# Gated mix of local attention and a squared-ReLU MLP: later row tiles of the first tokens loaded through ScalarE's queue, products over two token tiles in turn, no products on zeros

## The chip, the core and the metric

The kernel runs on one core of one Trainium2 chip. The metric is device time in microseconds: the median of several runs. One further execution is taken with the hardware profiler; its rows are what the text reads. PE is TensorE's matmul row, PEld its weight loads, DVE VectorE, ACT ScalarE, POOL GpSimd, SP SyncE.

## What is computed

For 2048 tokens of width 448 (float32) the reference mixes two branches with a gate per token:

```python
g = sigmoid((x * gate_w).sum(-1))
q, k, v = split(x @ wqkv)            # 16 heads of 28
a = softmax(q . k[pos - 2*j], j = 0..7) weighted v, @ wo     # window 8, dilation 2
b = relu(x @ w1 + b1)**2 @ w2 + b2   # 1792 hidden
out = g * a + (1 - g) * b
```

## The kernel before

Products are to be more exact than one pass of TensorE's fast float32 form (fp32r) gives. So every operand is split into a high part, rounded to fp32r, and a low part, the rest: `split_full` (L114) has ScalarE write the high part (L115) and VectorE subtract it for the low part (L116). A product of two operands is then three matmuls: high x high, high x low, low x high.

The 448 rows of the contraction are three row tiles of 128 (k = 0, 1, 2) and a last one of 64 that is held twice, in partitions 0 to 63 and 64 to 127. Tokens come transposed, in four chunks of 512 (`CH`), each of four token tiles of 128 (i = 0 to 3). The order on every engine is written out by hand; a planner's clock (`advance`, `at`, `when`) hands out splits, loads, stores and attention pieces as the products go on. A part of the work on one engine stands in a queue and waits in order.

The stretch that matters here is the start, up to the first 16 us:

- L103 clears one element (`none`), L618 a tile of zeros, and L620 runs 13 products (`WARM`) on these zeros.
- L625 to L632 issue the loads of the first chunk and its query weights, all on SP's queue. For each k: the weights' row tile (`wqraw0`, L627; 128 x 450, 450 because two columns of the gate stand beside the 448), then the tokens' row tile (`xraw0`, L632; 128 x 512, for k = 0 in two halves of 256 columns). For the last row tile the weights come in two parts (L630). Then come the weights of keys and values (L637, L640) and the second chunk (L554).
- L642 to L652 split what lands. For k = 0, 1, 2 ScalarE rounds the weights (L643, `wqh`), VectorE rounds the tokens (L645) and makes the weights' low part (L646, `wql`) and the tokens' low part (L647). For k = 0 the second half of the tokens is rounded by ScalarE (L649), with its low part on VectorE (L650). The last row tile goes through `split_full` (L115, L116).
- `qkv_first` (L246) then has the first query products. For each k and each token tile i it issues the three matmuls of that tile (L253): high x wqh, high x wql, low x wqh, all into the accumulator of tile i. Behind the twelve products of k it issues `FILL[k]` = 2, 1, 0 products on the zeros (L256). Everything later runs as pairs of 64 rows side by side (L184, `side_by_side`), first with the last row tile, for queries and keys.

The DMAs of the program take their completion semaphores in turn out of eight. So a ninth and a tenth load wait, before they are issued, for an earlier load with the same semaphore to land.

`none` (L102) is also the source of small ScalarE copies that let the next accumulation pass between the two halves of the rows (`turn`, L192).

Of the kernel before, what the change touches and what calls it, by code (L numbers as in the profile page):

```python
# [9 lines left out]
AF = mybir.ActivationFunctionType  # L10
# [4 lines left out]
P = 128  # L15
# [7 lines left out]
CH = 512  # L23
NQ = D + 2
# [23 lines left out]
DEFER = 2  # L48
ORDER = (3, 0, 1, 2)
WARM = 13  # L50
FILL = (2, 1, 0)
PP_BUFS = 4
ST_BUFS = 3
BT_BUFS = 8
# [3 lines left out]
def gated_mix_kernel(ctx: ExitStack, tc: tile.TileContext, xT, wqkv, w1, w2, wo, b1, b2, out):  # L58
    nc = tc.nc

    def f32(ap):
        return ap.bitcast(F32)
# [37 lines left out]
    biasp = ctx.enter_context(tc.tile_pool(name="biasp", bufs=1))  # L100
    b1z = biasp.tile([P, 16], F32, name="b1z")
    b1t, none = b1z[:, :NF], b1z[0:1, 15:16]  # L102
    nc.vector.memset(none, 0.0)  # L103

    ctx.enter_context(tc.manual_schedule())
    nc.gpsimd.memset(mask, 0.0)
# [24 lines left out]
    def x_tiles(c, pool):  # L131
        return X([pool.tile([P, 2, CH], F32R, tag=f"x{j}", name=f"x{c}_{j}") for j in range(4)])
# [9 lines left out]
    def ps(tag, name):  # L142
        return psum.tile([P, 512], F32, tag=tag, name=name, bufs=4)
# [20 lines left out]
    def block(b):  # L164

        o = (0, NP, NP + D)[b]
        return slice(o, o + ncols(b))
# [45 lines left out]
    def full(x, acc, tl, b, ks=range(3)):  # L213
        sl, n = slice(tl * P, tl * P + P), block(b)
        r = []
        for k in ks:
            r += [(acc, x.h[k][:, sl], wqh[:, k, n]), (acc, x.h[k][:, sl], wql[:, k, n]),
                  (acc, x.l[k][:, sl], wqh[:, k, n])]
        return r

    def last(x, acc, tl, b):

        sl = slice(tl * P, tl * P + P)
        n = block(1) if b == 2 else slice(0, ncols(b))
        h, l = w7h[:, n], w7l[:, n]
        return [(acc, x.x7[:, sl], h), (acc, x.x7[:, sl], l), (acc, x.x8[:, sl], h)]

    def accs(c, b, tls, tags):
        return [Acc(t, f"qkv{c}_{tl}_{b}", ncols(b)) for t, tl in zip(tags, tls)]

    def run(c, todo, steps):


        a = 0
        for e, done, *turns in steps:
            side_by_side(todo[0][a:e], todo[1][a:e])
            while a < e:
                advance(min(12, e - a) * MM448)
                a = min(a + 12, e)
            for t in turns:  # L240
                t() if callable(t) else turn(*t)
            for b, tl, acc in done:
                assert acc.todo == 0
                qkv_evacuate(acc.pt, c, tl, b)

    def qkv_first(x):  # L246

        four = range(4)
        q = accs(0, 0, four, "bbbb")
        for k in range(3):  # L250
            for i in four:
                for j, (acc, a, w) in enumerate(full(x, q[i], i, 0, (k,))):
                    nc.tensor.matmul(acc.pt[:, :NQ], a, w, start=k == j == 0, stop=False)  # L253
            advance(12 * MM448)
            for _ in range(FILL[k]):
                nc.tensor.matmul(warm[:, :2 * P], zero[:, :P], zero, start=True, stop=True)  # L256
        for acc in q:
            acc.todo = 3
        k = accs(0, 1, four, "mmmm")
        t = [sum((last(x, a[i], i, b) for i in four), []) for b, a in ((0, q), (1, k))]  # L260
        f = [full(x, k[i], i, 1) for i in four]
        run(0, [t[0] + f[0] + f[1] + f[2] + f[3], t[1] + f[2] + f[3] + f[0] + f[1]],
            [(3, [(0, 0, q[0])], (k[0], k[0])),
             (12, [(0, i, q[i]) for i in (1, 2, 3)], (k[1], k[1])),
             (24, [], (k[0], k[2])), (33, [], (k[1], k[3])),
             (39, [(1, 0, k[0]), (1, 2, k[2])]), (48, [(1, 1, k[1]), (1, 3, k[3])])])
        v = accs(0, 2, four, "bbbb")
        f, l = [full(x, v[i], i, 2) for i in four], [last(x, v[i], i, 2) for i in four]
        run(0, [f[0] + l[0] + f[2] + l[2] + f[1] + f[3], f[1] + l[1] + f[3] + l[3] + f[0] + f[2]],
            [(15, [], (v[0], v[1])), (24, [], (v[2], v[3])),  # L270
             (33, [(2, 0, v[0]), (2, 1, v[1])]), (42, [(2, 2, v[2]), (2, 3, v[3])])])
# [195 lines left out]
    def advance(dt):  # L467
        clock["pe"] += dt
        while due := [x for x in later if x[0] <= clock["pe"]]:
            item = min(due, key=lambda x: x[0])  # L470
            later.remove(item)
            item[1]()
        if not clock["on"]:
            clock["att"] = clock["pe"]
            return
        while clock["att"] < clock["pe"]:
            try:
                r = next(att)
            except StopIteration:
                clock["on"] = False  # L480
                return
            if r is None:
                clock["att"] = clock["pe"]
                return
            clock["att"] += r


    def raw_tile(name):
        return rawp.tile([P, 4, 512], F32, tag="raw", name=name)
# [126 lines left out]
    warm = ps("m", "warm")  # L616
    zero = prodp.tile([P, 2 * P], F32R, tag="pp", name="zero", bufs=PP_BUFS)
    nc.vector.memset(f32(zero), 0.0)  # L618
    for _ in range(WARM):
        nc.tensor.matmul(warm[:, :2 * P], zero[:, :P], zero, start=True, stop=True)  # L620

# [2 lines left out]
    rx = raw_tile("xraw0")  # L624
    for k in range(4):  # L625
        if k < 3:
            nc.sync.dma_start(raws[0][:, k, :NQ], wqkv[0, :, k])  # L627
        else:
            for b, rows in ((0, slice(0, 64)), (1, slice(64, P))):
                nc.sync.dma_start(raws[0][rows, k, :NQ], wqkv[b, rows, k])  # L630
        for cols in ((slice(0, 256), slice(256, CH)) if k == 0 else (slice(0, CH),)):
            nc.sync.dma_start(rx[:, k, cols], xT[0, :, k, cols])  # L632

    for b, tag in ((1, "k"), (2, "v")):
        raw = attp.tile([P, 3, D], F32, tag=tag, name=f"wqraw{b}")
# [5 lines left out]
    x = x_tiles(0, xap)  # L641
# [77 lines left out]
    for c in range(4):  # L719
        x = xs[c]  # L720
        if c == 0:
            qkv_first(x)
        else:
            qkv_two(x, c, 0, copies=c == 3)
            qkv_two(x, c, 2, (mlp_one, mlp_two) if c == 3 else (), c == 3)
        if c == 1:
            st_["spilled"] = 0
            clock["on"] = True
            clock["att"] = clock["pe"] - 1.0
            advance(0.0)  # L730
        if c == 3:
            st_["spilled"] = 1
# [266 lines left out]
    for g in range(2, 2 * NF):  # L999
        i, f = g // (NF // 2), g % (NF // 2) * 2  # L1000
# [4 lines left out]
        if not f:  # L1005
            x, slots = X([nxt[j][0] for j in range(4)]), [nxt[j][1] for j in range(4)]
# [111 lines left out]
```

## Time and profile before

| | us |
|---|---|
| median of 3 runs | 418.29 (418.14 to 418.49) |
| the profiled execution | 418.03 |
| its span, first to last instruction | 416.1 |
| PE busy | 409.4 |
| DVE, ACT, POOL busy | 256.0, 207.8, 268.7 |
| first product of real data starts (L253) | 4.74 |
| first product of L184 starts | 13.57 |

Times in the views are counted from the span's start. A matmul's busy time overlaps with the next one's, so the distance from start to start tells the pace, not the mean duration. A row of the timeline has the start, the duration, engine, line, operation, out<-in, shape and count; in brackets how long the engine was idle before it and what ended the wait. A row of the view of windows has the busy time of PE, PEld, DVE, ACT and POOL in the stretch, then the granted clock of TensorE, the mean busy share of the core's 16 DMA engines, and GB/s.

### The profile page before, as it was taken

What the parts mean: (1) busy time and instruction counts of PE and PEld (TensorE: products, weight loads), DVE (VectorE), ACT (ScalarE), POOL (GpSimd) and SP (SyncE); (2) the same over time, 40 slices, a digit from 0 to 9 for tenths busy, and PEclk for the clock granted to TensorE, in tenths of its full rate; (3) what the DMA queues carried; (4) which work ended last, traced back from release to release, by engine and by line L of the source; (5) the groups of instructions that cost most, each with busy time, mean ns of one, the idle gap of its engine ahead of it and who ended that gap; (6) DMA issues with size and microseconds to landing.
All of it is one profiled execution on the core that took longest, in us unless ns stands there. A gap on an engine that the chain in (4) does not pass through costs nothing.

```text
span 416.1 us, 9332 instructions
## 1 busy us (share of the span) xinstructions
PE 409.4 (98%) x3844; PEld 377.4 (91%) x3844; DVE 256.0 (62%) x403; ACT 207.8 (50%) x471; POOL 268.7 (65%) x167
## 2 busy tenths in 40 slices
PE   8999999999999999999999999999999999999995
PEld 7999999999999999888888888989898888888994
DVE  4520522276676767777656797879586677882343
ACT  3641655288766565444565535444653253346630
POOL 0000000874988999999989898999899986940000
PEclk9999999999999999999999999999999999999999
DMA  7999799979164307554112659765146512178204
GB/s 227 359 339 317 225 365 284 366 248 329 48 204 177 127 2 256 207 183 150 30 56 100 223 162 260 195 145 149 33 154 199 213 46 84 51 184 129 83 2 177
DMA packets 65323, 73.76 MB, mean 177 GB/s; under 512 B 32320, under 2 KB 58368, under 8 KB 64896
## 3 DMA queue, kind: packets, MB, share of 16 engines
q1 hardware_dynamic: 65280, 73.16, 54.5%
q8 instruction: 30, 0.49, 0.5%
q14 instruction: 13, 0.11, 0.1%
HBM read 45.71 MB, written 28.25 MB: 178 GB/s over the span
## 4 chain that ended last, share of the span: by engine, by line
PE 95%; DVE 2%; DMA 1%; ACT 1%; issue 0%; DVEq 0%; SPq 0%
PE b L184 32%; PE h L184 31%; PE qkv L184 21%; PE a L184 8%; PE qkv L253 2%; DVE lg L329 1%; DMA xraw<-xT 1%; DVE bt L795 0%; DVE w1l L511 0%; DVE h L608 0%; ACT copy L506 0%; ACT st L203 0%; DVE w17l L511 0%; DVEq L1113 0%; DVE o L346 0%
## 5 line engine op out<-in xcount | busy, mean ns | idle before, releaser
L328 POOL TENSOR_TENSOR qk<-q,k 128x896 f32<-128x896 f32 x64 | 135.1, 2151 | 85.6 <-DMA k<-k_d 80.6
L335 POOL TENSOR_TENSOR av<-lg,v 128x896 f32<-128x896 f32 x64 | 119.9, 1972 | 6.2 <-DVE lg L329 4.7
L184 PE MATMUL qkv<-wqh,x 64*128 64x448 f32 (+1 forms) x528 | 89.7, 362 | 0.1
L608 DVE TENSOR_TENSOR h<-h,h 128x512 fp32r<-128x512 f32 x56 | 38.4, 688 | 61.3 <-ACT h L611 61.0
L184 PEld LDWEIGHTS qkv<-wqh,x 64*128 64x128 f32 x528 | 69.5, 184 | 1.4 <-DVE qkv L194 0.5
L184 PE MATMUL qkv<-wql,x 64*128 64x448 f32 (+1 forms) x264 | 69.2, 361 | 0.0
L329 DVE TENSOR_REDUCE lg<-qk 128x32 f32<-128x896 f32 x64 | 67.3, 1075 | 2.7 <-POOL qk L328 2.7
L184 PE MATMUL b<-w2ah,h 64*128 64x448 f32 x448 | 67.6, 360 | 0.4 <-DVE h L608 0.4
L343 DVE TENSOR_REDUCE o<-av 128x112 f32<-128x896 f32 x64 | 66.5, 1070 | 1.7 <-POOL av L335 1.5
L184 PE MATMUL b<-w2bh,h 64*128 64x448 f32 x448 | 66.9, 360 | 0.0
L609 ACT ACTIVATE h<-h,b1z 128x512 f32<-128x512 f32 x56 | 36.7, 655 | 43.6 <-PE h L184 43.6
L184 PEld LDWEIGHTS b<-w2ah,h 64*128 64x128 f32 x448 | 43.2, 184 | 3.7 <-DVE h L608 1.0
L184 PEld LDWEIGHTS b<-w2bh,h 64*128 64x128 f32 x448 | 42.8, 184 | 3.3 <-ACT h L560 0.3
L203 ACT ACTIVATE st<-qkv 128x448 f32<-128x448 f32 x48 | 24.5, 543 | 36.6 <-PE qkv L184 30.2
L184 PE MATMUL b<-w2al,h 64*128 64x448 f32 x224 | 41.5, 358 | 0.0
L184 PE MATMUL b<-w2bl,h 64*128 64x448 f32 x224 | 41.1, 358 | 0.0
L184 PEld LDWEIGHTS qkv<-wql,x 64*128 64x128 f32 x264 | 40.6, 184 | 0.4
L610 ACT ACTIVATE h<-h 128x512 fp32r<-128x512 f32 x56 | 33.5, 598 | 1.7
L611 ACT ACTIVATE h<-h 128x512 f32<-128x512 f32 x56 | 33.3, 594 | 0.0
L184 PE MATMUL h<-x,w1h 64*128 64x512 f32 x168 | 30.1, 386 | 0.0
L560 ACT ACTIVATE h<-h 128x4 fp32r<-128x4 f32 (+1 forms) x35 | 7.2, 206 | 43.3 <-PE b L184 43.2
L184 PE MATMUL h<-x0b,w1h 64*128 64x512 f32 x168 | 28.1, 386 | 0.0
(130 smaller groups left out, 706.1 us busy)
## 6 DMA issues: line engine op xcount, KB each, us to landing
k<-k_d SPq DMA_DIRECT2D x8, 840.0 KB, 6.4
v<-v_d SPq DMA_DIRECT2D x8, 840.0 KB, 4.8
x_d<-x SPq DMA_DIRECT2D x12, 512.0 KB, 5.3
q_d<-st SPq DMA_DIRECT2D x8, 448.0 KB, 5.2
k_d<-st SPq DMA_DIRECT2D x8, 448.0 KB, 4.1
v_d<-st SPq DMA_DIRECT2D x8, 448.0 KB, 7.0
w1raw<-w SPq DMA_DIRECT2D x4, 896.0 KB, 10.0
q<-q_d SPq DMA_DIRECT2D x8, 448.0 KB, 3.6
```

The costliest lines, as they stand in the source:

```text
L184: nc.tensor.matmul(acc.pt[:, :acc.n], a[rows], w[rows], start=acc.todo == acc.all, stop=acc.todo == 1)
L203: nc.scalar.activation(st[:, :, t % 2], pt[:, :D].rearrange("p (g c) -> p g c", g=G), AF.Copy)
L253: nc.tensor.matmul(acc.pt[:, :NQ], a, w, start=k == j == 0, stop=False)
L328: nc.gpsimd.tensor_mul(pr, q[:, s:s + 1].to_broadcast([P, W, C]), k[:, s:s + W])
L329: pending.append(lambda: nc.vector.tensor_reduce(lg[:, s], pr.rearrange("p w (h d) -> p w h d", h=HG), axis=AX.X, op=ALU.add))
L335: nc.gpsimd.tensor_mul(pr.rearrange("p (h d) w -> p w h d", h=HG), lg[:, s][:, :, :, None].to_broadcast([P, W, HG, DH]), v[:, s:s + W].rea ...
L343: nc.vector.tensor_reduce(o[:, g * C:(g + 1) * C], pr, axis=AX.X, op=ALU.add)
L560: nc.scalar.activation(ap, f32(ap), AF.Copy)
L608: nc.vector.tensor_sub(hl, pt, f32(hh))
L609: ops += [lambda pt=pt, r=r: nc.scalar.activation(pt, pt, AF.Relu, bias=b1t[:, f + r:f + r + 1]), lambda pt=pt, hh=hh: nc.scalar.activatio ...
L610: lambda pt=pt, hh=hh: nc.scalar.activation(hh, pt, AF.Square),
L611: lambda pt=pt, r=r, low=low: (nc.scalar.activation(pt, pt, AF.Square), at(delays[r], low))]
```

## The change

Three things change, all in the start.

1. The tokens' row tiles k = 1, 2 and the last one are loaded through ScalarE's queue in place of SP's. The weights and the two halves of k = 0 stay on SP's queue. Ahead of these issues ScalarE copies the one element `none` onto itself, its first operation with an activation function; to that end the memset of `none` moves behind that of the zeros.
2. In `qkv_first` the products of two token tiles are issued in turn: high x wqh for tiles 0 and 1, then high x wql for both, then low x wqh for both, then the same for tiles 2 and 3. Before, all three of a tile were issued ahead of the next tile's.
3. The products on zeros behind each k (`FILL`) are left out.

In the built program the order of all later instructions is the same on every engine. ScalarE's third load waits for the first weight tile to land (the semaphore that both use), and ScalarE's first split stands behind it; SP's second part of the last weights waits for the first half of the tokens. On SP the loads of the key and value weights move up by the issues that left.

```diff
--- before.py
+++ after.py
@@ -48,7 +48,6 @@
 DEFER = 2
 ORDER = (3, 0, 1, 2)
 WARM = 13
-FILL = (2, 1, 0)
 PP_BUFS = 4
 ST_BUFS = 3
 BT_BUFS = 8
@@ -100,7 +99,6 @@
     biasp = ctx.enter_context(tc.tile_pool(name="biasp", bufs=1))
     b1z = biasp.tile([P, 16], F32, name="b1z")
     b1t, none = b1z[:, :NF], b1z[0:1, 15:16]
-    nc.vector.memset(none, 0.0)
 
     ctx.enter_context(tc.manual_schedule())
     nc.gpsimd.memset(mask, 0.0)
@@ -248,12 +246,11 @@
         four = range(4)
         q = accs(0, 0, four, "bbbb")
         for k in range(3):
-            for i in four:
-                for j, (acc, a, w) in enumerate(full(x, q[i], i, 0, (k,))):
-                    nc.tensor.matmul(acc.pt[:, :NQ], a, w, start=k == j == 0, stop=False)
+            for two in ((0, 1), (2, 3)):
+                for j, prods in enumerate(zip(*(full(x, q[i], i, 0, (k,)) for i in two))):
+                    for acc, a, w in prods:
+                        nc.tensor.matmul(acc.pt[:, :NQ], a, w, start=k == j == 0, stop=False)
             advance(12 * MM448)
-            for _ in range(FILL[k]):
-                nc.tensor.matmul(warm[:, :2 * P], zero[:, :P], zero, start=True, stop=True)
         for acc in q:
             acc.todo = 3
         k = accs(0, 1, four, "mmmm")
@@ -616,6 +613,7 @@
     warm = ps("m", "warm")
     zero = prodp.tile([P, 2 * P], F32R, tag="pp", name="zero", bufs=PP_BUFS)
     nc.vector.memset(f32(zero), 0.0)
+    nc.vector.memset(none, 0.0)
     for _ in range(WARM):
         nc.tensor.matmul(warm[:, :2 * P], zero[:, :P], zero, start=True, stop=True)
 
@@ -628,8 +626,13 @@
         else:
             for b, rows in ((0, slice(0, 64)), (1, slice(64, P))):
                 nc.sync.dma_start(raws[0][rows, k, :NQ], wqkv[b, rows, k])
-        for cols in ((slice(0, 256), slice(256, CH)) if k == 0 else (slice(0, CH),)):
-            nc.sync.dma_start(rx[:, k, cols], xT[0, :, k, cols])
+        if k == 0:
+            for cols in (slice(0, 256), slice(256, CH)):
+                nc.sync.dma_start(rx[:, k, cols], xT[0, :, k, cols])
+
+            nc.scalar.activation(none, none, AF.Copy)
+        else:
+            nc.scalar.dma_start(rx[:, k], xT[0, :, k])
 
     for b, tag in ((1, "k"), (2, "v")):
         raw = attp.tile([P, 3, D], F32, tag=tag, name=f"wqraw{b}")
```

## The prediction

> **What bounds the kernel now.** I read the page first: the share of each engine, and the chain of work that ended last.
>
> ```profile
> span 416.1 us, 9332 instructions
> ...
> PE 409.4 (98%) x3844; PEld 377.4 (91%) x3844; DVE 256.0 (62%) x403; ACT 207.8 (50%) x471; POOL 268.7 (65%) x167
> ...
> PE 95%; DVE 2%; DMA 1%; ACT 1%; issue 0%; DVEq 0%; SPq 0%
> ```
>
> TensorE (PE) sets the end. Second, the view of waits for PE alone, to see whether time won at the start can be lost again:
>
> ```profile
> PE b L184 <- DVE h L608: 0.4, 1, 0.4
> PE qkv L253 <- DVE x L645: 0.4, 1, 0.4
> ```
>
> Behind the first microseconds PE waits once, for 0.4 us. A start that is earlier by T therefore ends the kernel earlier by T, give or take that wait. Third, the chain over the first 16 us, where the change lies (start, duration, what):
>
> ```profile
> 4.29 0.30 DVE x L645
> ...
> 4.74 3.51 PE qkv L253 x12
> 8.24 0.23 PE warm L256 x2
> 8.48 2.58 PE qkv L253 x12
> 11.06 0.12 PE warm L256
> 11.18 2.46 PE qkv L253 x12
> ```
>
> Three groups of 12 products, one for each row tile k, take 3.51, 2.58 and 2.46 us. The third is undisturbed: 2.46/12 = 0.205 us each. So the start holds at most (3.51 - 2.46) + (2.58 - 2.46) + 0.23 + 0.12 = 1.52 us that a better order could take, 0.36% of the kernel. Fourth, the timeline says what that is. PE, and the low parts it reads:
>
> ```profile
> 1.23 3.14 PE L620 MATMUL warm<-zero 128*128 128x256 f32 x13 [1.23 <-DVE zero L618]
> 4.50 0.62 DVE L646 TENSOR_TENSOR wql<-wqraw,wqh 128x450 fp32r<-128x450 f32 x1
> 4.74 0.71 PE L253 MATMUL qkv<-wqh,x 128*128 128x450 f32 x1 [0.37 <-DVE x L645]
> 5.04 0.42 DVE L647 TENSOR_TENSOR x<-xraw,x 128x256 fp32r<-128x256 f32 x1
> 5.25 0.67 PE L253 MATMUL qkv<-wql,x 128*128 128x450 f32 x1
> 5.72 0.88 PE L253 MATMUL qkv<-wqh,x 128*128 128x450 f32 x2
> 6.43 0.36 PE L253 MATMUL qkv<-wql,x 128*128 128x450 f32 x1
> 6.63 0.57 PE L253 MATMUL qkv<-wqh,x 128*128 128x450 f32 x2
> ```
>
> The first products start 0.51 and 0.47 us apart, the next two take (6.43 - 5.72)/2 = 0.355 us each, all later ones about 0.2. The first two gaps end with wql (5.12) and with the low part of x (5.46): waits. The 0.355 is something else, a PE that runs slow until about 6.4 us. The page's granted clock is full here, so only the spacing tells it.
>
> **The change, part by part.**
>
> *No products on zeros.* The 0.23 + 0.12 = 0.35 us of L256 lie in the chain. They go at full value if the operands behind them are ready, which the next step decides. The memset of one element, moved behind that of the zero tile, lets the first 13 products on zeros start about 0.1 us earlier; they end earlier too, and the first real product doesn't depend on them: nothing gained, and 0.1 us more idle time before it.
>
> *Two token tiles in turn.* Every accumulator keeps its products, only their order changes: high x high for both tiles, then with wql for both, then the low part of x for both. A low part is thus asked for two and four products after the first instead of one and two. In the first group, at 0.37 us each (0.355 with a little to spare), wql is wanted at 4.74 + 0.74 = 5.48 and x's low part at 6.2: both are there. The lost time is (0.51 - 0.37) + (0.47 - 0.37) = 0.24 us. It lies in the slow stretch; if that ends at the same moment as before, 0.24 us there is worth 0.24 x 0.205/0.37 = 0.13. I take 0.13, and keep 0.24 as the other end. In the second group:
>
> ```profile
> 7.14 0.43 DVE L645 CAST x<-xraw 128x512 fp32r<-128x512 f32 x1 [0.80 <-DMA xraw<-xT]
> 7.49 0.62 DVE L646 TENSOR_TENSOR wql<-wqraw,wqh 128x450 fp32r<-128x450 f32 x1
> 8.03 0.68 DVE L647 TENSOR_TENSOR x<-xraw,x 128x512 fp32r<-128x512 f32 x1
> 8.76 0.30 PEld L253 LDWEIGHTS qkv<-wqh,x 128*128 128x128 f32 x2 [0.26 <-DVE x L647]
> ```
>
> The low part of x is done at 8.71 and the weight load of the third product waits 0.26 us for it; the group is 2.58 - 2.46 = 0.12 us over. With both steps it would begin near 8.24 - 0.13 = 8.1 and want wql (8.11 by now) at 8.5 and the low part at 8.9. So the wait goes even if no load lands any sooner: 0.12. The third group waits for nothing now, and neither does what follows:
>
> ```profile
> 9.80 0.69 DVE L647 TENSOR_TENSOR x<-xraw,x 128x512 fp32r<-128x512 f32 x1
> 11.07 0.68 DVE L116 TENSOR_TENSOR x<-xraw,x 128x512 fp32r<-128x512 f32 x1
> 13.57 0.47 PE L184 MATMUL qkv<-w7h,x 64*128 64x450 f32 x2
> ```
>
> Moved up 0.6 us the third group wants its last low part near 11.3 (there at 10.49), and L184 starts near 13.0 and wants the last row tile's (there at 11.75): about 0.8 us and over 1 us of cover. Sum of these two steps: 0.35 + 0.13 + 0.12 = 0.60 us.
>
> *Three loads through ScalarE's queue.* By the sum above PE doesn't need them earlier. What they can cost stands in front of ScalarE's first split and on the shared DMA engines:
>
> ```profile
> 0.74 1.28 ACT L643 ACT_TABLE_LOAD   x1 [0.74 <-PEq L1110]
> 0.90 0.27 DVE L618 MEMSET zero<- 128x256 f32 x1
> 2.60 0.43 SPq L632 DMA_DIRECT2D xraw<-xT  x1
> 3.50 0.58 ACT L643 ACTIVATE wqh<-wqraw 128x450 fp32r<-128x450 f32 x1 [1.47 <-DMA wqraw<-wqkv]
> 5.28 0.58 SPq L632 DMA_DIRECT2D xraw<-xT  x1
> 5.47 0.42 ACT L649 ACTIVATE x<-xraw 128x256 fp32r<-128x256 f32 x1 [1.39 <-DMA xraw<-xT]
> 6.09 0.58 ACT L643 ACTIVATE wqh<-wqraw 128x450 fp32r<-128x450 f32 x1 [0.21 <-DMA wqraw<-wqkv]
> ```
>
> The added copy of one element pulls the table load to the front, where it stands already. No row shows an issue by ScalarE; SP's take 0.43 to 0.58. Two of the three fit between 1.2 (the memset of the copied element, now behind that of the zero tile) or 2.02 (end of the table load) and 3.50. The third waits, in the built program, for the first weight tile to land, that is until 3.50, and ScalarE's split of that tile is queued behind it: it would start at 3.93 to 4.08 and end at 4.51 to 4.66. PE's first product waits for x's high part until 4.59 anyway, so this costs from nothing to 0.06 us, and wql moves to at most 5.3, before 5.48. The split that follows on ScalarE, x's second half (5.47), isn't touched.
>
> On the wire it is less certain (busy time of PE, PEld, DVE, ACT, POOL; then granted clock, DMA share, GB/s):
>
> ```profile
> 2.50:3.00 0.50, 0.50 (x4) 0.50 (x4) 0.00 (x0) 0.00 (x0) 0.00 (x0) 1.00 0.94 333
> 3.50:4.00 0.50, 0.50 (x5) 0.50 (x3) 0.00 (x0) 0.50 (x1) 0.00 (x0) 1.00 0.36 86
> 5.50:6.00 0.50, 0.50 (x2) 0.49 (x2) 0.09 (x1) 0.38 (x1) 0.00 (x0) 1.00 1.02 355
> ```
>
> The engines are full at 2.5 to 3 and again from 4.5 on, with a hole at 3 to 4. ScalarE's first load, 256 KB, is issued 0.6 to 1.3 us sooner than SP issues it now (2.60), beside the first weight tile and the first halves of x, which the first product needs. At 333 GB/s its 0.262 MB are 0.79 us: the delay of the first product is between 0 (all of it fits the hole) and 0.79. The hole, half a microsecond at a third of the rate or so, takes most of it: I choose 0.2 us, worth 0.2 x 0.205/0.37 = 0.11 while PE is slow. The second weight tile, now behind half of ScalarE's bytes, lands later than 6.09 by up to the same 0.79; its split would then end at 7.46, wql near 8.1, for a use near 8.5: hidden.
>
> [...]
>
> **Sum:** -0.60 + 0.11 = about -0.5 us. The profiled execution took 418.03 us (span 416.1 and 1.9 around it), which gives 417.5; it is 0.26 below the median 418.29 of runs that differ by 0.35, and against that median the forecast is 417.8. Its own ends: -0.60 - 0.11 (the full 0.24) = -0.7, and with 0.79 us of delay in place of 0.2, -0.17; with 0.2 for the run, 417.4 to 418.3.
>
> **Rivals.** *Crowded out.* The first load of ScalarE goes fully ahead of the first halves of x: first product at 5.5, price 0.79 x 0.205/0.37 = 0.44, and the second half of x and the second weight tile late as well, some 0.2 us of new waits in the second group. Sum -0.60 + 0.64 = 0: 418.3. For it: both queues are busy from 2.5 on. Against: the hole.
>
> *Slow clock for longer (slower).* PE runs slow from 1.23 until about 6.4, 5.2 us of work with one hole of 0.37 in it. If the hole before the first product grows (0.1 from the earlier zeros, 0.2 to 0.8 from the loads) so far that the count starts again at the first product, the rise comes at 4.94 + 5.2 = 10.1, 3.7 us later, and costs 3.7 x (1 - 0.205/0.355) = 1.56: -0.5 + 1.56 = +1.1, so 419.4. [...] Against: the waits of 0.24 go, and they broke the same stretch.
>
> *Clock rises sooner (faster).* If those waits held the rise back, it comes at the first product at the earliest: 1.66 us of slow time less, worth 1.66 x (1 - 0.205/0.355) = 0.70. Then -1.2: 417.1. Against: the hole ahead of the first product stays.
>
> [...]
>
> *The loads land no earlier at all.* That leaves the forecast as it is.
>
> **How the numbers follow.** Forecast 0.59, crowded out 0.12, slow clock 0.15, early clock 0.14. A measurement of this kernel tells about 0.2%, 0.84 us, from no change. Of the forecast 0.10 lies beyond -0.84 (its -0.7 with the scatter of runs), so faster 0.14 + 0.10 = 0.24; slower 0.15; same 0.49 + 0.12 = 0.61. The range goes from the early clock, 417.0, over crowded out with its scatter, to 418.8, and leaves out the slow clock and a few per cent of the others.
>
> **What would show it.** First product within 0.3 us of 4.74; the first two groups without waits inside; spacing 0.2 from about 6.4 on; L184 first at 13.0 to 13.2 instead of 13.57; ScalarE's first split at about 4.0. Wrong, if the first product starts after 5.3, if spacings of 0.36 last beyond 7, if the second group waits for wql or x, or if L184 starts 0.5 us earlier and the end doesn't.

## The result, and the profile after

The changed kernel takes 421.27 us (median of 12 runs, 418.68 to 423.94) beside 418.22 us for the kernel before (12 runs, 417.69 to 418.72). The ratio is 1.0074, interval 1.0051 to 1.0096: slower, where the forecast was 0.5 us faster. The scatter is part of the result: 5.3 us between the executions of the changed kernel, 1.0 between those of the kernel before. The profiled execution is the slowest of the twelve, 423.94 us, with a span of 421.9 us. Two lines number differently now: the first products stand in L252 (L253 before), the paired ones in L182 (L184).

From the page of the changed kernel: the new DMA queue, q10, with what ScalarE issues (packets, MB, share of 16 engines), and the chain's shares by engine.

```profile
q10 hardware_dynamic: 432, 0.79, 0.7%
...
PE 87%; DMA 7%; DVE 2%; ACT 2%; issue 1%; SPq 0%; DVEq 0%; ACTq 0%
```

DMA has grown from 1% to 7% of the chain. That share isn't the loss, since the chain now also runs through loads that cost PE little; what PE loses stands in the view of its waits (us in total, times, longest):

```profile
PE qkv L252 <- DVE x L648: 1.8, 1, 1.8
PE qkv L182 <- DVE qkv L192: 1.7, 1, 1.7
...
PE qkv L252 <- ACT x L652: 0.6, 1, 0.6
```

Before, PE waited 0.4 us for its first product; now 1.8, and again 0.6 in the middle of the first group. The 1.7 us at L182 are a later wait, taken up below. The chain of the first 24 us:

```profile
1.65 7.15 DMA xraw<-xT
...
9.30 7.84 PE qkv L252 x30
17.14 6.88 PE qkv L182 x63
```

The load issued at 1.65, the second half of the first tokens, still on SP's queue and still SP's third, lands at 8.80. Before, its reader started at 5.47. The timeline shows what came between (start, duration, engine, line; ACTq is ScalarE's issuing of DMAs):

```profile
1.20 0.86 ACTq L635 DMA_DIRECT2D xraw<-xT  x2
...
2.03 0.20 ACT L633 ACTIVATE b1z<-b1z 1x1 f32<-1x1 f32 x1
...
5.65 0.29 DVE L648 CAST x<-xraw 128x256 fp32r<-128x256 f32 x1 [4.51 <-DMA xraw<-xT]
...
9.37 0.58 ACT L646 ACTIVATE wqh<-wqraw 128x450 fp32r<-128x450 f32 x1
...
10.96 1.64 PE L252 MATMUL qkv<-wqh,x 128*128 128x450 f32 x4
...
12.85 0.98 PE L252 MATMUL qkv<-wqh,x 128*128 128x450 f32 x4
```

Three things are to be seen. ScalarE sends its first two loads at 1.20, when SP begins to send the halves of the first tokens: the copy that stands ahead of them in the program runs only at 2.03, and the issues didn't wait for it to run. The first half of the tokens is there at 5.65 (4.29 before), the second weight tile is split from 9.37 (6.09 before). And PE is slow far longer: four products at 10.96 take 1.64 us, four at 12.85 take 0.98; one starts every 0.37 us in the former and every 0.205 in the latter. Before, the pace changed near 6.4.

The first paired product starts at 17.07 in place of 13.57, 3.5 us late, and the span is longer by 5.8 (421.9 beside 416.1). The other 2 us come in one place near 93 us.

### The profile page after: what moved, and what is told of

The parts are those of the page before. It is cut to its first block, busy times and chain, and to the rows that moved or that the text cites. A ratio compares the mean times of both kernels' runs of the same rounds, so it can differ in the third digit from the quotient of the medians.

```text
span 421.9 us, 9327 instructions
## 1 busy us (share of the span) xinstructions
PE 411.4 (98%) x3841; PEld 375.7 (89%) x3841; DVE 255.5 (61%) x403; ACT 207.7 (49%) x472; POOL 269.0 (64%) x167
## 4 chain that ended last, share of the span: by engine, by line
PE 87%; DMA 7%; DVE 2%; ACT 2%; issue 1%; SPq 0%; DVEq 0%; ACTq 0%
PE b L182 32%; PE h L182 31%; PE qkv L182 15%; PE a L182 8%; DMA w1raw<-w 2%; DMA k_d<-st 2%; PE qkv L252 2%; DMA xraw<-xT 2%; DVE lg L326 1%; ACT st L201 1%; DVE bt L798 0%; DVE w1l L508 0%; DVE h L605 0%; ACT w17h L113 0%; SPq L207 0%
## 5 line engine op out<-in xcount | busy, mean ns | idle before, releaser
L182 PE MATMUL qkv<-wqh,x 64*128 64x448 f32 (+1 forms) x528 | 89.5, 362 | 1.8 <-DVE qkv L192 1.7
L182 PEld LDWEIGHTS qkv<-wqh,x 64*128 64x128 f32 x528 | 69.4, 185 | 3.2 <-DVE qkv L192 2.6
L182 PE MATMUL b<-w2ah,h 64*128 64x448 f32 x448 | 67.0, 360 | 0.4 <-DVE h L605 0.4
L182 PE MATMUL qkv<-wql,x 64*128 64x448 f32 (+1 forms) x264 | 67.2, 361 | 0.0
L182 PE MATMUL b<-w2bh,h 64*128 64x448 f32 x448 | 66.4, 360 | 0.0
L182 PEld LDWEIGHTS b<-w2ah,h 64*128 64x128 f32 x448 | 42.4, 184 | 4.0 <-DVE h L605 1.0
L182 PEld LDWEIGHTS b<-w2bh,h 64*128 64x128 f32 x448 | 42.3, 184 | 3.4 <-ACT h L557 0.3
L182 PE MATMUL b<-w2al,h 64*128 64x448 f32 x224 | 40.9, 358 | 0.0
L182 PE MATMUL b<-w2bl,h 64*128 64x448 f32 x224 | 40.8, 358 | 0.0
L182 PEld LDWEIGHTS qkv<-wql,x 64*128 64x128 f32 x264 | 40.2, 184 | 0.3
L182 PE MATMUL h<-x,w1h 64*128 64x512 f32 x168 | 28.9, 386 | 0.0
L182 PE MATMUL h<-x1b,w1h 64*128 64x512 f32 x168 | 28.2, 386 | 0.0
```

The costliest lines, as they stand in the source:

```text
L182: nc.tensor.matmul(acc.pt[:, :acc.n], a[rows], w[rows], start=acc.todo == acc.all, stop=acc.todo == 1)
```

## The experiments

Theory A: the loads through ScalarE's queue crowd out the tiles that the first products need, and what else changes is a gain. Rival theory B: the order of products, or the missing zeros, keep PE slow, and the loads do nothing. Both leave open how much of A is late data and how much is PE's slow pace. "L184 from" is the start of the paired products in the chain of each profile.

| kernel | median us | before, same chip | ratio, interval | L184 from | span |
|---|---|---|---|---|---|
| before | | | | 13.64 | 416.1 |
| changed | 421.27 | 418.22 | 1.0074 (1.0051 to 1.0096) | 17.14 | 421.9 |
| e1_sp_turn_nofill | 417.46 | 418.07 | 0.9982 (0.9971 to 0.9993) | 12.94 | 415.4 |
| e2_act_loads_only | 422.62 | 418.07 | 1.0091 (1.0065 to 1.0117) | 18.55 | 421.2 |
| e3_turn_only | 417.86 | 418.07 | 0.9989 (0.9978 to 1.0000) | 13.15 | 415.7 |
| e4_after_warm21 | 420.21 | 418.07 | 1.0046 (1.0029 to 1.0062) | 15.66 | 418.3 |
| e5_before_warm8 | 418.60 | 417.94 | 1.0018 (1.0009 to 1.0027) | 14.22 | 416.9 |
| e6_act_loads_later | 420.94 | 417.94 | 1.0074 (1.0057 to 1.0092) | 15.12 | 418.1 |
| e8_after_again | 421.70 | 417.94 | 1.0091 (1.0067 to 1.0116) | 15.99 | 418.6 |
| e9_first_tokens_on_act | 417.75 | 417.94 | 0.9992 (0.9983 to 1.0000) | 13.30 | 416.1 |
| e10_one_act_load | 419.53 | 418.07 | 1.0028 (1.0014 to 1.0042) | 14.02 | 416.7 |
| e11_turn_warm16 | 417.38 | 418.07 | 0.9983 (0.9974 to 0.9992) | 12.54 | 415.1 |
| e12_sp_again | 417.48 | 418.07 | 0.9987 (0.9975 to 0.9999) | 12.94 | 415.6 |

**e1: the change without its loads.** The kernel before, with the new order of products and without `FILL`:

```diff
-            for i in four:
-                for j, (acc, a, w) in enumerate(full(x, q[i], i, 0, (k,))):
-                    nc.tensor.matmul(...)
+            for two in ((0, 1), (2, 3)):
+                for j, prods in enumerate(zip(*(full(x, q[i], i, 0, (k,)) for i in two))):
+                    for acc, a, w in prods:
+                        nc.tensor.matmul(...)
             advance(12 * MM448)
-            for _ in range(FILL[k]):
-                nc.tensor.matmul(warm[:, :2 * P], zero[:, :P], zero, start=True, stop=True)
```

> The kernel before with products in turn and no products on zeros between the groups; all loads stay on SP. Theory A (the loads through ScalarE crowd the first tiles out, the rest of the change is good): first product at 4.74, L184 near 13.0, time 0.4 to 0.7 us under the kernel before, about 417.6. Theory B (products in turn, or the missing products on zeros, keep PE slow, the loads do nothing): slower by 2 to 4 us, like the changed kernel.

Measured: 417.46, 0.61 us under the kernel before. Theory B falls. The timeline of PE shows a full pace from the second pair of products on, not from 6.4 on:

```profile
4.22 0.83 PE L254 MATMUL qkv<-wqh,x 128*128 128x450 f32 x2
4.89 0.57 PE L254 MATMUL qkv<-wql,x 128*128 128x450 f32 x2
5.29 1.18 PE L254 MATMUL qkv<-wqh,x 128*128 128x450 f32 x4
```

What it wins there it can't keep. The chain now goes through the load of the second row tile, issued at 2.60 and landed at 6.98; PE has caught up with the loads, and the paired products start only 0.70 earlier.

```profile
2.60 4.38 DMA xraw<-xT
...
7.59 5.35 PE qkv L254 x24
```

**e12: e1 repeated, unchanged.**

> The fastest experiment again (loads on SP, in turn, no products on zeros between the groups), unchanged, beside the kernel with 16: 0.4 to 0.7 us under the kernel before, as the first time.

Measured: 417.48, 0.59 us under. In its profile the pace is full from the second pair on as well, and its chain goes through the second half of the first tokens.

**e3: the order alone**, `FILL` kept.

> The kernel before with only the products in turn. Theory A: 0.13 + 0.12 = 0.25 us faster, about 418.0. Theory B, if the turn is the cause: 1 us slower or more.

Measured: 417.86, 0.21 us under the kernel before; the interval touches 1. So of e1's 0.6 about a third is the order. In its chain the first two groups take 3.41 and 2.53 us, where the kernel before has 3.51 and 2.58; the second still waits for the low part of the tokens. Its pace is a surprise beside e1. Until 7.6 us PE has the same products to do in both, yet here they stay slow until about 6.3:

```profile
4.17 1.00 PE L254 MATMUL qkv<-wqh,x 128*128 128x450 f32 x2
4.96 0.95 PE L254 MATMUL qkv<-wql,x 128*128 128x450 f32 x2
5.71 1.26 PE L254 MATMUL qkv<-wqh,x 128*128 128x450 f32 x4
6.82 0.56 PE L254 MATMUL qkv<-wql,x 128*128 128x450 f32 x2
```

**e2: the loads alone.** Old order, `FILL` kept, the loads, the copy ahead of them and the moved memset as in the changed kernel:

```diff
-        for cols in ((slice(0, 256), slice(256, CH)) if k == 0 else (slice(0, CH),)):
-            nc.sync.dma_start(rx[:, k, cols], xT[0, :, k, cols])
+        if k == 0:
+            for cols in (slice(0, 256), slice(256, CH)):
+                nc.sync.dma_start(rx[:, k, cols], xT[0, :, k, cols])
+            nc.scalar.activation(none, none, AF.Copy)
+        else:
+            nc.scalar.dma_start(rx[:, k], xT[0, :, k])
```

> The kernel before with only the three loads moved to ScalarE's queue; the old order of products and the products on zeros stay. Theory A: first product near 6, second half of the first tokens landing after 7.5, time 2 to 4 us over the kernel before with a scatter of several us. Theory B: within 0.3 us of the kernel before.

Measured: 422.62, 4.6 us over, a little more than expected. The loads are the loss (e6 below keeps the copy and the memset, and its first product is early); the rest of the change takes about 1 us off it (421.27, and 421.70 in e8), though the intervals overlap. In this execution the clock that was granted to TensorE falls once more after it had risen, and the window view shows it behind the five busy times:

```profile
4.50:7.90 3.40, 1.85 (x6) 1.05 (x6) 1.16 (x3) 0.00 (x0) 0.00 (x0) 1.00 1.03 300
8.00:14.70 6.70, 5.40 (x15) 4.88 (x16) 5.40 (x11) 4.07 (x8) 0.00 (x0) 0.50 0.82 259
```

PE was busy for 1.85 of 3.40 us while it waited for tokens, and the clock then stood at half for some 6.8 us, until 14.77. In the second row 15 products take 5.40 us, 0.36 each.

**e4: the changed kernel with PE kept at work.** `WARM = 21` in place of 13.

> The changed kernel with 21 products on zeros ahead in place of 13, so that PE is at work until about 6 and the hole before the first product closes. If half of the loss is PE's slow clock that the hole prolongs: spacing 0.2 from about 6.5 on, and 1 to 2 us less than the changed kernel, 419 to 420. If the loss is only that the data land late: no change, 421 to 422.

Measured: 420.21, 1.06 us under the changed kernel and just above what was expected. The tokens land as late as there (first products and the second wait from its timeline), but the pace is fast at once, two products in 0.48 us from 5.97 on and two more from 6.45 on:

```profile
5.97 0.64 PE L252 MATMUL qkv<-wqh,x 128*128 128x450 f32 x2 [0.21 <-DVE x L648]
6.45 0.65 PE L252 MATMUL qkv<-wql,x 128*128 128x450 f32 x2
6.93 0.57 PE L252 MATMUL qkv<-wqh,x 128*128 128x450 f32 x2
9.31 0.68 PE L252 MATMUL qkv<-wqh,x 128*128 128x450 f32 x2 [1.80 <-ACT x L652]
```

So from e1 to the changed kernel, 417.46 to 421.27 = 3.8 us, some 2.75 (e4 less e1) are late data, and about 1.1 in the middle of the runs the slow clock. (Each taken against the kernel before on its own chip, the second part is 0.9, and 1.6 with the four runs of e8.) The runs of e4 also lie closer: all but one of nine within 419.74 to 420.36.

**e5: the hole by itself.** The kernel before with `WARM = 8`; no load moves.

> The kernel before with 8 products on zeros ahead in place of 13: nothing else moves, the loads least of all, and PE stands idle from about 3.3 until the first product at 4.74, 1.4 us in place of 0.37. If a hole of that size costs PE its fast clock: spacings of 0.37 until 9 to 12 in most executions, and 1 to 2.5 us more, with a scatter. If the slow clock of the changed kernel had to do with the loads or the order alone: within 0.2 us of the kernel before.

Measured: 418.60, 0.66 us over, runs from 418.15 to 419.78 beside 417.58 to 418.45. The sign is as expected, the size less, and the slow spacing ends at 8.6, sooner than expected. In its profile the hole is 0.86 us, since the tokens came a little sooner, and two products still take 0.95 us at 7.51, where the kernel before has 0.56 to 0.58 from 6.4 on:

```profile
4.16 0.71 PE L253 MATMUL qkv<-wqh,x 128*128 128x450 f32 x1 [0.86 <-DVE x L645]
...
7.51 0.95 PE L253 MATMUL qkv<-wqh,x 128*128 128x450 f32 x2
...
9.48 0.56 PE L253 MATMUL qkv<-wqh,x 128*128 128x450 f32 x2
```

**e8: the changed kernel again**, for a second profile.

> The changed kernel once more, unchanged, for a second profile: the landings should repeat (first half of the first tokens near 5.6, second near 8.8), and the slow clock may differ, since the times scatter from 418.7 to 423.9. If the scatter comes from the landings instead, these differ by us.

Measured: 421.70 (420.29 to 423.16, four runs), its profiled run 420.49. The first half of the tokens repeats (first product at 6.12), the second lands at 7.81 in place of 8.80, and the clock goes another way: full for the first six products (1.53 us of work; 2.59 for the same six in the first profile), then half until 11.36.

```profile
4.50:7.90 3.40, 1.53 (x6) 0.97 (x6) 1.17 (x3) 0.06 (x1) 0.00 (x0) 1.00 1.01 333
8.00:11.30 3.30, 2.99 (x8) 2.69 (x9) 2.87 (x7) 1.83 (x4) 0.00 (x0) 0.50 0.84 248
```

The slow stretch is 3.41 us here (7.94 to 11.36) and 6.83 in e2 (7.94 to 14.77). So the two profiles of the changed kernel differ in both, in the landing of the second half by 1 us (8.80 and 7.81) and in when PE is slow (until 12.39 there, from 7.94 to 11.36 here). PE's wait near 93 us is absent.

**e6: the same loads on ScalarE's queue, later**, behind its first split:

```diff
         nc.scalar.activation(wqh[:, k, :NQ], raws[0][:, k, :NQ], AF.Copy)
+        if k == 0:
+            for j in (1, 2, 3):
+                nc.scalar.dma_start(rx[:, j], xT[0, :, j])
```

> The changed kernel with ScalarE's three loads issued behind its first split, at about 3.6, so that the first weights and the first tokens are on their way alone. Theory A (early issue puts 0.5 MB ahead of the first tokens): first product back at 4.2 to 4.8, the second half of the first tokens by 6; time at or under the kernel before, 417.5 to 418.3. If a second queue slows the loads whatever its order: second half of the first tokens after 7, time 420 or more.

Measured: 420.94, a miss of Theory A as I had put it. The first product is back at 4.18 and the second half of the tokens at 6.12, as expected, but the second row tile is now the one that is late. Chain:

```profile
3.46 5.73 DMA xraw<-xT
...
9.79 5.33 PE qkv L252 x24
```

It is issued at 3.46 and lands at 9.19; in the kernel before it was issued at 2.60 and read at 7.14. By 3.46 SP has sent the second and third weight tiles and a part of the last; the third lands at 7.73, ahead of the row tile that is needed sooner. I read this as a matter of what went out before a load and not of its queue; no run has the same late issue on SP's queue, so that isn't shown by itself.

**e9: two queues, first-needed first.** e1 with the halves of the first tokens on ScalarE's queue and everything else on SP's.

```diff
+        if k == 0:
+            nc.scalar.activation(none, none, AF.Copy)
+            for cols in (slice(0, 256), slice(256, CH)):
+                nc.scalar.dma_start(rx[:, k, cols], xT[0, :, k, cols])
+        else:
+            nc.sync.dma_start(rx[:, k], xT[0, :, k])
```

> Products in turn, none on zeros, as in the fastest experiment so far, with the two halves of the first tokens on ScalarE's queue and all else on SP's: two queues, but the first-needed tiles are the first in each. Theory A: first product at 4.2 to 4.8 and a time within 0.5 us of that experiment, 417.0 to 418.0. If two queues at once are what hurts: first product after 5.5 and 420 or more.

Measured: 417.75, 0.19 us under the kernel before, 0.3 over e1. First product at 4.77. In this run two queues at once cost a few tenths at most, within what the intervals leave open; they gained nothing.

**e10: one of the three loads**, row tile 1, through ScalarE's queue.

> The changed kernel with only the first of the three loads (row tile 1) on ScalarE's queue, the other two back on SP's behind their weights. If each early load of 0.26 MB on ScalarE's queue takes the place of one of SP's: the first half of the first tokens as late as in the changed kernel (5.4 to 5.7, first product near 6), the second half by 6 to 6.5 in place of 7.8 to 8.8; time between, 418.5 to 420. If the second queue itself slows every load: second half after 7.5, and 420.5 or more.

Measured: 419.53 (417.72 to 420.05), between. In the chain the first half of the tokens, issued at 1.20, lands after 4.82 us; it took 3.08 before:

```profile
1.20 4.82 DMA xraw<-xT
...
6.47 7.55 PE qkv L252 x36
```

The second half had landed by 6.22 here (before: 5.45, changed: 8.80). One load in front delays the first half by 1.7 us against the profile of the kernel before. That profile is a late one: in the five others with all these loads on SP's queue (e1, e3, e5, e11, e12) the first half lands at 3.59 to 3.76 in place of 4.27, so 2.3 us is nearer. A second load in front delays the second half by another 1.6 (e8) to 2.6 us. In this execution the pace was full although PE stood idle for 2.14 us: then 36 products follow without a wait, in 7.55 us or 0.21 each, and the first product's delay of 1.73 us leaves only 0.4 at the paired products. The profiled run, 418.57, is 1 us under the median, so the slower runs of e10 aren't explained by it.

**e11: a version that beats both.** e1 with 16 products on zeros ahead, so that there is no hole.

> All loads on SP, products in turn, none on zeros between the groups, and 16 products on zeros ahead in place of 13, which closes the hole before the first product (3 x 0.21 = 0.64 us against 0 to 0.37). If the hole still holds the clock back in some executions: 0.1 to 0.5 us under the same kernel with 13, and less scatter. If not: the first product is late by the 0.1 to 0.6 us that the zeros reach beyond the landing, and the time is equal or up to 0.3 us more.

Measured: 417.38, 0.69 us under the kernel before, and the runs lie within 416.96 to 417.98. Against e12 (417.48, with one run at 419.63) that is no difference that the medians tell. PE has no hole ahead of the real products: its chain goes from the zeros into them. In e12's profile there is none either (first product at 4.17, zeros until 4.37), so 16 had nothing to close there.

```profile
1.23 3.62 PE warm L619 x16
4.85 7.69 PE qkv L254 x36
```

## Why the prediction was wrong

**What held.** A start that was late by T ended late by T: in the profiles of all eleven experiments the span follows the start of the paired products within some 0.5 us (table, against the kernel before: e1 -0.7 and -0.7, e4 +2.0 and +2.2, e2 +4.9 and +5.1). The sum of the first two steps, 0.60 us for the missing zeros and the order of products, was measured alone at 0.61 and 0.59 (e1, e12), and the order's share, 0.25, as 0.21 (e3). ScalarE's first split starts at 3.81, for a forecast of about 4.0.

**The size held, the way to it less.** In the profiles of e1 and e12 the rival "Clock rises sooner" came true: full pace from about 4.9. It should have given 1.2 us and gave 0.6, since PE then waits for loads that the prediction took to be hidden (the second half of the first tokens in e12, the second row tile in e1). Neither of the two parts brought the early clock: e1 and e3 have the same products on PE until 7.6 us, and the pace rises near 4.6 in one (the first two products take 0.67 us, the next two 0.40) and near 6.3 in the other (four take 1.11 us from 5.71 on, the next two 0.39); so the waits that this rival blamed, which the new order takes out of both, weren't it either. The moment of the rise differs from one execution to another, also with the same products on PE (below), and I put it down to chance; no run shows what sets it. So the agreement of 0.60 with 0.61 and 0.59 is in part luck: the gaps closed less than the sum had it (0.15 us in the first two groups of e3's profile for 0.25), the clock helped, and late loads took some of it back.

**What failed** is the step "Three loads through ScalarE's queue", in its sentence "I choose 0.2 us" between 0 and 0.79 on the wire, and in its "isn't touched" for the second half of the first tokens, which thus had no term in the sum. The first product came 1.35 us late, the second half of the tokens 3.4 us and the second weight tile 3.3 us, where the step had at most 0.79 and "hidden". Two of its own signs of being wrong came: a first product after 5.3 (6.09), and spacings of 0.36 beyond 7 (until 12.4). Three things in it were wrong.

- The bound. It let only the first of ScalarE's loads go ahead, at the engines' full rate: 0.262 MB at 333 GB/s. Both that go out from 1.20 on land ahead, one before each half: the last marks on their semaphores come at 5.44 and 8.53, those of the halves at 5.63 and 8.81. The profile gives 4.2 us from issue to landing for the first of ScalarE's loads, beside 4.4 for SP's first half, issued in the same moment, and 6.9 for the second, beside 7.15 for SP's second half:

```profile
L635 ACTq DMA_DIRECT2D xraw<-xT x3: 335/384/445, 1.2 to 3.4; - x3
...
DMA to landing us min/median/max: 4.2/6.9/8.1
```

- The hole in the traffic at 3 to 4 us was taken for room that lets ScalarE's load pass at no cost. It is filled (before, then after the change), but of the 244 KB that start in it 164 are ScalarE's, and SP's own fall from 108 to 80. Later there is less traffic, not more: the two windows from 4 to 12 us have 274 and 225 GB/s after the change.

```profile
3.00:4.00 1.00, 1.00 (x7) 1.00 (x6) 0.00 (x0) 0.50 (x1) 0.00 (x0) 1.00 0.47 108
3.00:4.00 1.00, 1.00 (x7) 1.00 (x5) 0.00 (x0) 0.20 (x1) 0.00 (x0) 1.00 0.99 244
...
4.00:8.00 4.00, 2.25 (x7) 1.81 (x7) 1.16 (x3) 0.38 (x1) 0.00 (x0) 1.00 0.91 274
8.00:12.00 4.00, 3.38 (x9) 2.50 (x9) 2.72 (x6) 1.70 (x4) 0.00 (x0) 1.00 0.80 225
```

  e1 has 278 and 332 there. The second is lower, and in it SP's next loads, the six of L640 from 8.82 on, had waited for the late second half (queue's waits on SP: total, times, longest):

```profile
SPq L640 <- DMA xraw<-xT: 2.7, 1, 2.7
```

- "Crowded out" was priced with the first load alone, at 0.64, which made its sum 0; by e4, in which the clock is fast, the sum is 2.1 us over the kernel before, and the price (e4 less e1) 2.75.

That the loads would gain nothing was right: there was no gain (e2 is 4.6 us over the kernel before). What I drew for the delay was too little. The second queue, which starts early, doesn't stand behind the first one in the traces. In e10 one load delays mostly one half, in the changed kernel two delay both. And the packets of the changed kernel's trace can be counted by queue: from 3 to 5 us 159 start on SP's and 156 on ScalarE's, about as many on one as on the other. They carry 146 and 289 KB, since 143 of the former are rows of a half tile, 1 KB each, and 141 of the latter rows of a whole tile, 2 KB: with as many packets the queue with the longer rows moved twice the bytes. In the kernel before SP's queue alone moved 365 KB in that time. (From 5.5 to 7 us it is 268 packets to 49, so the equal counts don't last.)

Not all of the 3.4 us is explained by these counts. In the trace 16 marks come on the semaphore of the second half, between 5.64 and 8.81, eleven of them by 6.62, and its reader starts behind the last, at 8.83 (before: from 3.97 to 5.45, the reader at 5.47). In the middle they are about 1.5 us late, and the last few add the rest. Why those lag wasn't settled.

**The slow clock** was a rival with a chance of 0.15, taken as an alternative to "Crowded out"; in truth the two came together, since it is the late data that make the hole. Its price of 1.56 was of the right size: 1.5 us in the changed kernel's profile (paired products at 17.14, 15.66 in e4's). The reason given for it was not borne out. The prediction supposed a count that starts again at the first product once the hole is long enough; no run shows such a count, and e10 has a hole of 2.14 us with the full pace behind it.

What the runs show is stretches: a slow one of 3.41 us (e8) and one of 6.83 (e2), which is twice that. Each trace keeps the times at which the granted clock changed (before the first of them the window view prints 1.00). The first change is to the full clock, at 6.38 in the kernel before, 12.39 in the changed one, 4.60 in e1 and 6.29 in e3, and the spacing of products changes there too: 0.355 us before 6.43 and 0.2 from then on in the kernel before, 0.37 before 12.43 and 0.205 from then on in the changed one. In the traces of these two kernels the next change comes 409.60 us later, after the last products, and that is 120 times 3.413 us. From these records I estimated that the clock changed, where it did, at steps of 3.41 us, from a moment that differs between executions. The steps at which it didn't change aren't recorded; I laid them back and on from the changes that are. The half clock ahead of the first change is read from the spacing, and PE's busy time is that of the window view:

| stretch, us | run | PE at work in it, of 3.41 | clock in it, and after it |
|---|---|---|---|
| 2.16 to 5.57 | changed | 2.17 | half, half |
| 5.57 to 8.98 | changed | 2.59 | half, half |
| 8.98 to 12.39 | changed | 3.09 | half, full |
| 2.97 to 6.38 | before | 3.04 | half, full |
| 1.56 to 4.97 | e10 | 2.78 | half, full |
| 4.97 to 8.38 | e10 | 1.91 | full, full |
| 4.53 to 7.94 | e8 | 1.53 | full, half |
| 4.53 to 7.94 | e2 | 1.85 | full, half |

In these rows the half clock became full after 2.78 us of work or more and not after 2.59 or less, and the full clock was lost after 1.85 or less and kept after 1.91; in e6 it was kept after 1.87 (8.25 to 11.66). The hole of 0.37 us in the kernel before lies in the stretch with 3.04, and the clock rose at its end. e10's hole of 2.14 us (4.34 to 6.47) lies across two stretches, with 2.78 and 1.91, and the pace behind it was full; that this is why it cost nothing is my reading, and so is that the moments, which differ between executions, are one cause of the changed kernel's scatter. This ordering was found afterwards, no run was made to test it, and one stretch at the end of e9 (1.54, the clock stays full) doesn't fit, so PE's busy time as the profile has it can't be all that counts.

**What stays open.** In the changed kernel's first profile another 2 us arise near 93 us. The chain has it from a load of MLP weights, issued at 79.08 and landed at 89.51, through ScalarE's splits and VectorE to the memsets that PE waits for:

```profile
79.08 10.44 DMA w1raw<-w
...
94.96 0.05 DVE qkv L192 x2
```

Earlier ScalarE had stood idle for 3.79 us up to 50.47, for a store of v to free its staging tile (1.30 us in the kernel before). That the load was late for this reason is only argued, and why the store was slower in that execution wasn't settled. In the profiles of e2, e4 and e8, with the same loads at the start, PE doesn't wait there, so it belongs to the scatter of 418.7 to 423.9 and not to the median.

## What to carry to other kernels

At this start, which is bound by loads, moving the first-needed tiles to another engine's queue gained nothing (e9, 0.3 us over e1), and moving later ones there put them beside the first-needed and cost 4.6 us (e2). Before you move a load, ask which tiles will be on their way when the first-needed one goes out, and count every byte that any queue issues by then, here two loads of 0.26 MB for 2 to 3 us. An order of products that asks for the late operand last needs no load to move; here it gave 0.2 us, at the edge of what the runs can tell. While TensorE waits for first data, keep it at work until they are there: here a longer hole went with a slower pace later (about 1 us between the changed kernel and e4, 0.7 in e5), though not in e10's profile, with 2.14 us of hole, while behind the hole of 0.37 us in the kernel before the clock rose at 6.38.

## What the runs showed that I had not expected

- In three of these runs a DMA issue on ScalarE's queue came when the operation ahead of it had what it waits for, and didn't wait for that operation to end. In the changed kernel the issue at 1.20 precedes by 0.83 us the copy that stands in front of it and that runs at 2.03 behind the table load; it follows the memset that the copy waits for (done at 1.14; in e9 at 0.86, and the issue at 0.90). In e6 the issue comes at 3.46, as the split ahead of it starts, and not at its end (4.04). So the operation ahead held these loads back by its wait alone.
- ScalarE's issues took 0.34 to 0.45 us each in the changed kernel and 0.39 to 0.59 in e6; SP's of the same row tiles took 0.43 to 0.58 in the kernel before.
- With one of ScalarE's loads issued beside it, the first half tile of 128 KB took 4.4 us (changed) and 4.82 (e10) from issue to landing, in place of 3.08 (before) and 2.50 (e5); its neighbour, with two, took 6.16 (e8) to 7.17 us (e4) in place of 3.80 (before) and 3.96 (e12).
